# First blocks of 128, 128, 256, 256 and 256 tokens in a two-layer gated network behind a dynamic convolution, with earlier decoding of the weights and a new plan

## The chip, the core and the metric

One core of one Trainium2 chip runs the kernel. Its engines are TensorE (PE, with its weight loads shown apart as PEld), VectorE (DVE), ScalarE (ACT), GpSimd (POOL) and SyncE (SP, which here only issues transfers). The metric is the device time of one execution in microseconds, the median of the runs.

## What is computed

8192 tokens of 192 values pass through three steps. A causal convolution over 7 tokens has weights of its own for every token and head (a softmax of `weight_gen`). Then come two layers of 192 to 2048 to 192, the first with a rational function between its products, the second with a clipped product:

```python
def _moe_ref(x, w_in, w_out, a, b):
    h = x @ w_in
    h2 = h * h
    h3 = h2 * h
    P = a[0] + a[1] * h + a[2] * h2 + a[3] * h3
    Q = 1.0 + np.abs(b[0]) * np.abs(h) + np.abs(b[1]) * h2
    return (P / (Q + 1e-06)) @ w_out

def _moe2_ref(x, w_in, w_out):
    h = x @ w_in
    g = h * np.clip(h + 3.0, 0.0, 6.0) / 6.0
    return g @ w_out
```

The weights of both layers come as float64 and are decoded to float32 on the core.

## The kernel before

The tokens lie as 128 partitions of 64 rows, and a block is some of these rows for all partitions: `BL` (L46) has two blocks of 256 tokens and 15 of 512, called b0 to b16 here. A slice is the part of a block's 2048 hidden values that fills one 512-column bank: two groups of 128 hidden values for 256 tokens, one for 512. So a block of 256 has 8 slices and one of 512 has 16.

For a block the steps are these. The convolution's products (`conv_mul`, L171, on POOL, the first also on DVE) and sums (`conv_sum`, DVE) make the input; `xT` transposes it on PE, and `x_hi` (ACT) and `x_lo` (DVE) split it into a rounded part and a rest, since the products run on split operands. `in1` (L295) multiplies a slice of layer one with five matrix multiplications per group of 128 hidden values. The rational function takes a chain on ACT, DVE and POOL that ends with `pool_m` and `pool_lo` on POOL (L378, L389), which writes `glo`. Its denominator has two forms: `whole` slices add it up on DVE (L321), the others (through `act_u`, the Abs form) multiply it on POOL (L341). `out1` (L407) adds the slice to the block's output in the bank pair `y1`, again with five multiplications per group. When the last slice is in, `mid_y`, `mid_f`, `mid_head`, `head_lo`, `mid_tail` and `tail_lo` (L227 to L265) fold the output and split it for layer two: `in2` (L427), `act_r2`, `dve_g2`, then `out2` (L447) on unsplit float32, and `evac` to the output. `y1` is single, so the next block's `out1` waits for `tail_lo`.

The weights come in 28 jobs (`order`, L642): a load into one of `ST` = 8 buffers, then `low` and `scale` (ACT, or DVE for scale), `join` and `sign` (DVE), and for all but `o2` a cut into `hi` (ACT) and `lo` (POOL or DVE, L532). The first two loads are issued from ACT's queue, the others from SP's.

The order on every engine is written out by `plan()` (L820): a list scheduler with a cost and a due time for each step, made of the constants at L600 to L630 (`T` is the period of a slice). Engines take their instructions strictly in that order. Where PE has nothing to do in the plan, `idle_mm` (L398) puts in filler multiplications of the identity; on the chip they run in their place, whether the gap is there or not.

Of the kernel before, what the change touches and what calls it, by code (L numbers as in the profile page):

```python
# [8 lines left out]
F32 = mybir.dt.float32  # L9
# [10 lines left out]
def kernel(  # L20
# [12 lines left out]
    nc = tc.nc  # L33
# [12 lines left out]
    BL = [2, 2] + [4] * 15  # L46
    B0 = [sum(BL[:b]) // 2 for b in range(len(BL))]
    BT = [n * P for n in BL]
    BV = [n // 2 for n in BL]
    BF = [GW // n for n in BT]  # L50
    BMAX = max(BT)
    UB = [(b, v) for b, n in enumerate(BV) for v in range(n)]
# [52 lines left out]

    def load_chunk(c):
        t = two.tile([P, ROWS, D], F32, tag="x", name="x")
        first = c * CT - (K - 1)
        neg = max(0, -first)
        cut_at = ROWS - 2 if c == 0 else ROWS  # L110
        segs = [(0, P, neg, cut_at)]
# [7 lines left out]
        for p0, p1, r0, r1 in segs:  # L119
            src = bass.AP(  # L120
                tensor=xf.tensor,
                offset=xf.offset + (first + p0 * R + r0) * D,
                ap=[[R * D, p1 - p0], [1, (r1 - r0) * D]],
            )
            nc.sync.dma_start(out=t[p0:p1, r0:r1].rearrange("p r d -> p (r d)"), in_=src)
        xch[c] = t
# [36 lines left out]
    NS = 3  # L163
# [7 lines left out]
    def conv_mul(u, i, z, e="DVE"):  # L171
        eng = nc.vector if e == "DVE" else nc.gpsimd
        c, t = divmod(u * 2 + i, CT)
# [25 lines left out]
    def x_dup(u):  # L199
        t = xc[u]  # L200
        nc.scalar.activation(out=t[:, :, D:], in_=t[:, :, P:D], func=AF.Copy)

    def xT(u):
        t = xc.pop(u)
        ps = bank(("xT", u), [P, 2, HB], "xT")
        for s in range(2):
# [4 lines left out]
    def x_hi(u):  # L211
        b, v = UB[u]
        if v == 0:
            xin[0, b] = [
                two.tile([P, 2, BMAX], F32R, tag=n, name=n)[:, :, : BT[b]] for n in ("xh0", "xl0")
            ]
        xh = xin[0, b][0]
        nc.scalar.activation(out=xh[:, :, v * HB : (v + 1) * HB], in_=xps[u], func=AF.Copy)

    def x_lo(u):  # L220
        b, v = UB[u]
        xh, xl = (t[:, :, v * HB : (v + 1) * HB] for t in xin[0, b])
# [4 lines left out]
    def mid_y(b):  # L227
        ysb[b] = one.tile([P, BMAX], F32, tag="ys", name="ys")[:, : BT[b]]
        for h in range(2):
            nc.scalar.activation(  # L230
                out=ysb[b][h * 64 : (h + 1) * 64],
                in_=y1[b][(1 - h) * 64 : (2 - h) * 64, 1, : BT[b]],
# [3 lines left out]
    def mid_head(b):  # L236
        n = BT[b]
# [711 lines left out]
```

## Time and profile before

| | us |
|---|---|
| median of 3 runs | 1306.07 (1305.97 to 1306.53) |
| the profiled execution | 1305.82 |
| its span, first to last instruction | 1304.0 |
| PE busy, share of the span | 1281.1, 98% |
| DVE, ACT, POOL busy | 1143.5, 1069.3, 984.3 |
| granted TensorE clock, mean | 0.996 |

PE's instructions are pipelined, so a busy PE isn't a PE at its best: two multiplications that overlap count once, and one that runs at half clock counts fully. What PE achieves is read from the distance between starts. A filler counts as busy too. An instruction of float32 on unsplit operands stands twice in the trace (fillers and `out2`), a transpose once.

### The profile page before, as it was taken

Reading aid. Unit: us, or ns where it says so; the run is one execution under the profiler, and the core shown is the slowest. Engines: PE = TensorE matmul, PEld = TensorE weight load, DVE = VectorE, ACT = ScalarE, POOL = GpSimd, SP = SyncE. Lnnn points to the kernel's source line nnn. Section 1 sums busy time; section 2 is a strip of 40 time slices with the busy share of each in tenths; the row PEclk is TensorE's granted clock in tenths of the full one; section 3 lists DMA queues with packets and bytes.
Section 4 is the critical chain, followed back from the end, with each engine's and each line's share of the span. In section 5 each row is a group of like instructions: output and inputs, shape, how many; then the busy total and the mean of one; then the engine's idle time right before and its main releaser. Section 6 shows DMA issues by size and latency. Waiting matters only on the chain.

```text
span 1304.0 us, 18918 instructions
## 1 busy us (share of the span) xinstructions
PE 1281.1 (98%) x6640; PEld 1127.2 (86%) x6640; DVE 1143.5 (88%) x1774; ACT 1069.3 (82%) x1893; POOL 984.3 (75%) x811
## 2 busy tenths in 40 slices
PE   8889999999999999999999999999999999999998
PEld 8888878888889888898988889898888988888898
DVE  7899999999899898988989898898989889896931
ACT  6998989889788797978879798887979888797931
POOL 7998897978878787777968777787877778575620
PEclk9989999999999999999999999999999999999999
DMA  7440100110100101010010101001010000000000
GB/s 237 147 144 1 37 11 1 41 37 5 36 12 7 40 1 47 1 37 10 8 40 1 47 1 37 10 8 40 1 43 1 7 7 7 8 1 13 1 13 13
DMA packets 16263, 37.64 MB, mean 29 GB/s; under 512 B 1964, under 2 KB 12586, under 8 KB 16168
## 3 DMA queue, kind: packets, MB, share of 16 engines
q1 hardware_dynamic: 15864, 35.39, 8.3%
q10 hardware_dynamic: 304, 1.05, 0.3%
q8 instruction: 52, 0.85, 0.3%
q14 instruction: 43, 0.35, 0.1%
HBM read 30.14 MB, written 6.29 MB: 28 GB/s over the span
## 4 chain that ended last, share of the span: by engine, by line
PE 85%; ACT 7%; DVE 3%; POOL 2%; DMA 1%; issue 1%; SPq 0%; POOLq 0%; ACTq 0%
PE h L279 41%; PE y L454 24%; PE y L418 4%; PE y L421 4%; PE y L419 4%; PE y L420 4%; PE y L422 4%; ACT r L361 1%; ACT l L334 1%; ACT st L511 1%; ACT ys L230 1%; ACT r L356 1%; ACT w L316 1%; PE xT L207 1%; ACT v L311 1%
## 5 line engine op out<-in xcount | busy, mean ns | idle before, releaser
L389 POOL TENSOR_TENSOR glo<-w,r 128x512 fp32r<-128x512 f32 x256 | 331.0, 1295 | 186.5 <-PE y L422 113.5
L378 POOL TENSOR_TENSOR w<-w,ghi 128x512 f32<-128x512 f32 x256 | 330.9, 1295 | 44.1 <-DVE ghi L370 32.0
L454 PE MATMUL y<-wo,g 128*128 128x192 f32 x2048 | 352.1, 326 | 0.0
L454 PEld LDWEIGHTS y<-wo,g 128*128 128x128 f32 x2048 | 337.9, 190 | 8.5
L382 DVE SCALAR_TENSOR_TENSOR w<-h,acol,w 128x512 f32<-128x512 f32 x256 | 190.2, 744 | 34.1 <-POOL w L378 33.2
L437 ACT ACTIVATE g<-h 128x512 f32<-128x512 f32 x256 | 153.7, 600 | 71.1 <-PE h L279 69.0
L279 PE MATMUL h<-xh,wst 128*128 128x512 f32 (+1 forms) x544 | 206.1, 379 | 1.3 <-POOL wst L532 1.3
L279 PE MATMUL h<-xl,wst 128*128 128x512 f32 (+1 forms) x544 | 205.7, 378 | 0.1
L334 ACT ACTIVATE l<-h,acol 128x512 f32<-128x512 f32 x256 | 200.5, 783 | 2.5 <-PE h L279 2.5
L177 POOL TENSOR_TENSOR prod<-x,wk 128x672 f32<-128x672 f32 x127 | 189.4, 1503 | 17.3 <-DVE xc L192 12.1
L370 DVE SCALAR_TENSOR_TENSOR ghi<-h,acol,r 128x512 fp32r<-128x512 f32 x256 | 189.8, 744 | 10.9 <-PE y L420 3.9
L441 DVE SCALAR_TENSOR_TENSOR g<-g,h 128x512 f32<-128x512 f32 x256 | 174.1, 680 | 22.3 <-ACT g L437 20.7
L349 DVE SCALAR_TENSOR_TENSOR h<-l,acol,h 128x512 f32<-128x512 f32 x256 | 191.1, 749 | 2.4
L345 DVE TENSOR_TENSOR l<-h,l 128x512 f32<-128x512 f32 x256 | 174.0, 682 | 8.0 <-ACT l L334 4.7
L356 ACT ACTIVATE r<-w 128x512 f32<-128x512 f32 x256 | 161.2, 634 | 19.4 <-DVE w L321 15.3
L361 ACT ACTIVATE r<-r 128x512 f32<-128x512 f32 x256 | 161.7, 633 | 2.5
L321 DVE SCALAR_TENSOR_TENSOR w<-w,v 128x512 f32<-128x512 f32 x171 | 116.1, 679 | 22.3 <-ACT w L316 21.3
L311 ACT ACTIVATE v<-h,bab 128x512 f32<-128x512 f32 x171 | 112.9, 660 | 21.4 <-PE h L279 18.9
L316 ACT ACTIVATE w<-h,root 128x512 f32<-128x512 f32 x171 | 117.9, 690 | 7.8 <-DVE l L345 6.5
L279 PEld LDWEIGHTS h<-xh,wst 128*128 128x128 f32 x544 | 103.1, 189 | 20.8 <-POOL wst L532 1.5
L279 PEld LDWEIGHTS h<-xl,wst 128*128 128x128 f32 x544 | 102.9, 189 | 19.7 <-DVE xl L262 0.4
L341 POOL TENSOR_TENSOR w<-w,u 128x512 f32<-128x512 f32 x85 | 109.8, 1292 | 12.3 <-ACT w L327 10.6
(82 smaller groups left out, 2452.0 us busy)
## 6 DMA issues: line engine op xcount, KB each, us to landing
x<-in_x_dram SPq DMA_DIRECT2D x14, 960.0 KB, 4.7
st<-in_moe_w_out_dram SPq DMA_DIRECT2D x16, 384.0 KB, 3.3
out_dram<-osb SPq DMA_DIRECT2D x32, 192.0 KB, 1.8
st<-in_moe_w_in_dram SPq DMA_DIRECT2D x7, 512.0 KB, 4.7
wg<-in_weight_gen_dram SPq DMA_DIRECT2D x16, 112.0 KB, 2.0
st<-in_moe_w_in_dram SPq DMA_DIRECT2D x6, 256.0 KB, 4.1
x<-in_x_dram SPq DMA_DIRECT2D x1, 768.0 KB, 6.3
st<-in_moe_w_in_dram ACTq DMA_DIRECT2D x2, 256.0 KB, 5.7
```

The source lines that it names most:

```text
L177: eng.tensor_tensor(out=pr.rearrange("p (h g) k -> p k h g", g=G), in0=xch[c][:, t : t + K, hs].rearrange("p k (h g) -> p k h g", g=G), in ...
L279: nc.tensor.matmul(out=dst, lhsT=l[:, fs], rhs=r, start=(n == 0), stop=(n == len(seq) - 1), skip_group_check=True,)
L334: nc.scalar.activation(out=l, in_=h1[sl], func=AF.Identity, scale=acol[:, 3:4], bias=acol[:, 2:3])
L349: nc.vector.scalar_tensor_tensor(out=h, in0=e["l"], scalar=acol[:, 1:2], in1=h, op0=ALU.add, op1=ALU.mult)
L356: nc.scalar.activation(out=r, in_=e["w"], func=AF.Ln, bias=0.0 if whole(sl) else CEPS)
L361: nc.scalar.activation(out=r, in_=r, func=AF.Exp, scale=-1.0)
L370: nc.vector.scalar_tensor_tensor(out=ghi, in0=h, scalar=acol[:, 0:1], in1=e["r"], op0=ALU.add, op1=ALU.mult)
L378: nc.gpsimd.tensor_tensor(out=m, in0=m, in1=g1[sl][0].bitcast(F32), op=ALU.mult)
L382: nc.vector.scalar_tensor_tensor(out=m, in0=h1.pop(sl), scalar=acol[:, 0:1], in1=m, op0=ALU.add, op1=ALU.subtract)
L389: nc.gpsimd.tensor_tensor(out=glo, in0=e["m"], in1=e["r"], op=ALU.mult)
L441: nc.vector.scalar_tensor_tensor(out=g, in0=g, scalar=1.0, in1=h2.pop((b, q)), op0=ALU.min, op1=ALU.mult,)
L454: nc.tensor.matmul(out=y2[b, v][:, s, :], lhsT=g2[b, q][:, c : c + P], rhs=wo2[:, n, :], start=(n == 0 and s == 0), stop=(n == NF - 1), sk ...
```

## The change

- The blocks are now 128, 128, 256, 256, 256 and 14 of 512 tokens (b0 to b18). A block of 128 has 4 slices of four groups each, and its multiplications have 128 columns.
- `y1` becomes two tiles, `ya` and `yc`: a wide block has its head in one and its tail in the other, freed by `head_lo` and `tail_lo` apart; a block of 128 has both in one tile, and the two such blocks use a tile each.
- The order of the jobs takes layer one's weights first and in the order in which slices need them; a cut's rests are steps of their own; the due times of the jobs (`JP0`, `JPT`, `JPU`) stand closer together.
- The first x transfers are three instead of six; the last two rows of chunk 0 have a step of their own, and the memset of row 64 stands behind the transfer. The loads on ACT's queue stand ahead of the first exponential.
- `whole` takes half of the first 32 slices and two thirds of the others, where it took two thirds of all: 165 slices instead of 171.
- All constants of the plan are new, the bank limit of the small class is 4 instead of 3, and each part of `out2` waits only for the slices that it reads.

```diff
-    BL = [2, 2] + [4] * 15
-    B0 = [sum(BL[:b]) // 2 for b in range(len(BL))]
+    PRE = [1, 1, 2, 2, 2]
+    BL = PRE + [4] * ((R - sum(PRE)) // 4)
+    R0 = [sum(BL[:b]) for b in range(len(BL))]
...
-    UB = [(b, v) for b, n in enumerate(BV) for v in range(n)]
+    UB = [(b, v, R0[b] + 2 * v, min(2, n)) for b, n in enumerate(BL) for v in range(BV[b])]
...
     def load_chunk(c):
...
-        if neg:
-            for b in range(B):
-                p = b * S // R
-                nc.gpsimd.memset(t[p : p + 1, 0:neg, :], 0.0)
-                segs += [(p + 1, p + 16, 0, neg), (p + 16, p + S // R, 0, neg)]
-        if cut_at < ROWS:
-            segs.append((0, P, cut_at, ROWS))
...
+        if neg:
+            nc.gpsimd.memset(t[0:1, 0:neg, :], 0.0)
+            load_x(c, 16, P, 0, neg)
+            load_x(c, 1, 16, 0, neg)
+        load_x(c, 0, P, neg, ROWS if c else ROWS - 2)
+        for b in range(1, B if neg else 0):
+            nc.gpsimd.memset(t[b * P // B : b * P // B + 1, 0:neg, :], 0.0)
+
+    def load_rest():
+        load_x(0, 0, P, ROWS - 2, ROWS)
...
     def whole(sl):
-        return sl < QN and sl % QK in QS
+        return sl % QK in QS if sl < QE else sl % QL in QT
...
     def open_y1(b):
-        if b not in y1:
-            y1[b] = ps_y.tile([P, 2, GW], F32, tag="y1", name="y1")
+        if b in y1:
+            return
+        n = BT[b]
+        if tight(b):
+            tag = "ya" if b % 2 == 0 else "yc"
+            t = ps_y.tile([P, GW], F32, tag=tag, name="y1")
+            y1[b] = [t[:, :n], t[:, n : 2 * n]]
+            spare[b] = [t[:, GW - P :]]
+        else:
+            ts = [ps_y.tile([P, GW], F32, tag=tag, name="y1") for tag in ("ya", "yc")]
+            y1[b] = [t[:, :n] for t in ts]
+            spare[b] = [t[:, GW - P :] for t in ts if n < GW]
...
-    QN = 256
-    QK = 3
+    QE = 32
+    QK = 4
     QS = [0, 1]
+    QL = 3
+    QT = [0, 1]
...
+        ("pair", 0, 0), ("in", 0, 0), ("in", 0, 1), ("o1", 0), ("o1", 1), ("pair", 0, 2),
+        ("in", 0, 2), ("o1", 2), ("o1", 3), ("in", 0, 3), ("o1", 4), ("o1", 5), ("o1", 6),
+        ("o1", 7), ("pair", 1, 0), ("in", 1, 0), ("in", 1, 1), ("pair", 1, 2), ("in", 1, 2),
+        ("o2", 0), ("o2", 1), ("in", 1, 3), ("o2", 2), ("o2", 3), ("o2", 4), ("o2", 5),
+        ("o2", 6), ("o2", 7),
...
-            step("lo", flex, 0, "hi")
+            for i, m in enumerate({"in": [512], "pair": [512, 512], "o1": [256, 128]}[key[0]]):
+                cp, cd = 0.06 + m * 0.00234, 0.08 + m / 960
+                step(i, (("POOL", cp, 0.0), ("DVE", cd + 0.2, PEN)), 0, "hi")
...
-            take=[("y1", 1, [("head_lo", b), ("tail_lo", b)])] if q == 0 else [])
+            take=[] if q else [("ya" if b % 2 == 0 else "yc", 1, [("head_lo", b), ("tail_lo", b)])]
+            if tight(b) else [("ya", 1, [("head_lo", b)]), ("yc", 1, [("tail_lo", b)])])
```

In the new order PE has 480 multiplications of 128 columns, 720 of 256 and 3360 of 512 on split operands (before 0, 480 and 3600), as many `out2` and transposes as before, and 187 fillers (192).

On PE, where block 0's first output multiplication stands: before, behind the last multiplications of its fourth slice,

```order
L279 MATMUL h_449<-xl_234,win0hi 128x256
L279 MATMUL h_449<-xh_233,wst_82 128x256
L279 MATMUL h_449<-xl_234,wst_82 128x256
L279 MATMUL h_449<-xh_233,win0lo 128x256
L418 MATMUL y_168<-ghi,wo1h 128x256
L419 MATMUL y_168<-ghi,wo1l 128x256
L420 MATMUL y_168<-ghi,wo1s 128x256
L421 MATMUL y_168<-glo,wo1h 128x256
```

and now, behind the first slice of block 1 (`h_579`), with the transposes of block 2's first rows between them:

```order
L275 MATMUL h_579<-xh_355,wst_82 128x128
L275 MATMUL h_579<-xl_356,wst_82 128x128
L275 MATMUL h_579<-xh_355,win0lo 128x128
L212 MATMUL xT<-ident,xc 128x128
L213 MATMUL xT<-ident,xc 128x128
L212 MATMUL xT<-ident,xc 128x128
L213 MATMUL xT<-ident,xc 128x128
L414 MATMUL y_168<-ident 128x128 x5
L430 MATMUL y_168<-ghi,wo1h 128x128
L431 MATMUL y_168<-ghi,wo1l 128x128
L432 MATMUL y_168<-ghi,wo1s 128x128
```

The output multiplications have 128 columns instead of 256, and PE has taken in all four slices of block 0 and one of block 1 by then.

On POOL, its first instructions after the identity, before:

```order
L103 MEMSET ex 128x32
L115 MEMSET x 1x1152 x2
L177 TENSOR_TENSOR prod<-x,wk 128x7x96 x4
L532 TENSOR_TENSOR wst_82<-st,wst_82 64x512 x2
L532 TENSOR_TENSOR win0lo<-st,win0hi 128x512
L177 TENSOR_TENSOR prod<-x,wk 128x7x96
L532 TENSOR_TENSOR win0lo<-st,win0hi 128x512
L177 TENSOR_TENSOR prod<-x,wk 128x7x96
L532 TENSOR_TENSOR win0lo<-st,win0hi 128x512
L177 TENSOR_TENSOR prod<-x,wk 128x7x96
L378 TENSOR_TENSOR w<-w,ghi 128x512
L389 TENSOR_TENSOR glo<-w,r_312 128x512
```

and now:

```order
L105 MEMSET ex 128x32
L122 MEMSET x 1x1152
L127 MEMSET x 1x1152
L544 TENSOR_TENSOR wst_82<-st,wst_82 64x512
L181 TENSOR_TENSOR prod<-x,wk 128x7x96 x4
L544 TENSOR_TENSOR win0lo<-st,win0hi 128x512
L544 TENSOR_TENSOR wo1l<-st,wo1h 128x256
L544 TENSOR_TENSOR wo1s<-st,wo1s 128x2x64
L181 TENSOR_TENSOR prod<-x,wk 128x7x96
L544 TENSOR_TENSOR wo1l<-st,wo1h 128x256
L544 TENSOR_TENSOR wo1s<-st,wo1s 128x2x64
L181 TENSOR_TENSOR prod<-x,wk 128x7x96
```

The first half of the cut of `wst` moved ahead of the convolution's products, and cuts of layer one's output weights (`wo1l`, `wo1s`) stand between those products; before, the first `glo` came as the last of these rows, and now it stands 20 rows further on.

On ACT, its first instructions, before:

```order
L902 ACT_TABLE_LOAD
L142 ACTIVATE ex<-wg 128x32x7
L475 DMA st<-in_moe_w_in_dram 64x1024 x2
L475 DMA st<-in_moe_w_in_dram 128x1024
L796 ACTIVATE bab<-bcol 128x2
L511 ACTIVATE st<-st 128x512
L507 ACTIVATE dt<-st 128x512
L802 ACTIVATE root<-root 128x1
```

and now:

```order
L938 ACT_TABLE_LOAD
L487 DMA st<-in_moe_w_in_dram 64x1024 x2
L487 DMA st<-in_moe_w_in_dram 128x1024
L146 ACTIVATE ex<-wg 128x32x7
L523 ACTIVATE st<-st 128x512
L519 ACTIVATE dt<-st 128x512
L523 ACTIVATE st<-st 128x512
L519 ACTIVATE dt<-st 128x512
L543 ACTIVATE wst_82<-st 64x512 x2
L543 ACTIVATE win0hi<-st 128x512
L832 ACTIVATE bab<-bcol 128x2
```

The three loads moved ahead of the exponential `ex`, and `bab`, which reads the coefficients `bcol`, moved behind the decoding of the first two jobs.

## Rows read from the trace of the kernel before

**Rows 1.** The page, part 1: busy us, share of the span, instructions.

```profile
PE 1281.1 (98%) x6640; PEld 1127.2 (86%) x6640; DVE 1143.5 (88%) x1774; ACT 1069.3 (82%) x1893; POOL 984.3 (75%) x811
```

**Rows 2.** By stage: length, then PE, PEld, DVE, ACT, POOL busy, granted clock, DMA.

```profile
20.00:80.00 60.00, 51.61 (x418) 48.74 (x416) 54.91 (x91) 57.50 (x116) 58.12 (x60) 1.00 0.53 169
80.00:120.00 40.00, 37.64 (x258) 34.64 (x259) 38.22 (x66) 38.55 (x73) 33.62 (x29) 0.92 0.17 52
120.00:190.00 70.00, 69.75 (x389) 62.71 (x388) 69.39 (x109) 62.70 (x113) 64.26 (x54) 1.00 0.07 22
190.00:200.00 10.00, 7.24 (x23) 5.25 (x24) 9.48 (x15) 8.75 (x16) 9.42 (x8) 0.83 0.00 0
```

**Rows 3.** By stage, PE's instructions on the identity alone: length, busy (count), clock.

```profile
20.00:120.00 100.00, 33.50 (x272) 0.97 0.39 122
```

**Rows 4.** Timeline of PE: start and length in us, line, count merged.

```profile
23.77 0.28 PE L279 MATMUL h<-xh,win0lo 128*128 128x256 f32 x1
...
24.37 0.28 PE L279 MATMUL h<-xh,win0lo 128*128 128x256 f32 x1
24.49 2.28 PE L402 MATMUL y<-ident 128*128 128x128 f32 x19
```

**Rows 5.** The chain that ended last, its longest pieces: start, length, count.

```profile
1262.73 17.01 PE h L279 x75
1279.74 20.82 PE y L454 x128
```

**Rows 6.** PE's groups by form, 200 to 1240 us: count | busy, mean ns.

```profile
L454 PE MATMUL y<-wo,g 128*128 128x192 f32 x1689 | 291.6, 326 | 0.0
...
L208 PE MATMUL xT<-ident,xc 128*128 128x128 f32 x52 | 12.7, 272 | 0.0
```

**Rows 7.** Timeline of PE's weight loads around 32 us, behind a wait.

```profile
32.25 0.19 PEld L279 LDWEIGHTS h<-xh,wst 128*128 128x128 f32 x1 [1.53 <-POOL wst L532]
32.35 0.19 PEld L279 LDWEIGHTS h<-xl,wst 128*128 128x128 f32 x1
```

**Rows 8.** Timeline of POOL: first products, first cut, first and eighth glo.

```profile
7.61 5.09 POOL L177 TENSOR_TENSOR prod<-x,wk 128x672 f32<-128x672 f32 x3 [4.16 <-DMA x<-in_x_dram]
...
15.66 2.67 POOL L532 TENSOR_TENSOR wst<-st,wst 64x512 fp32r<-64x512 f32 x2 [0.89 <-POOL prod L177]
...
28.79 1.28 POOL L389 TENSOR_TENSOR glo<-w,r 128x512 fp32r<-128x512 f32 x1 [1.06 <-DVE w L382]
...
76.39 1.28 POOL L389 TENSOR_TENSOR glo<-w,r 128x512 fp32r<-128x512 f32 x1
```

**Rows 9.** POOL's groups by form, the whole run: count | busy, mean ns.

```profile
L177 POOL TENSOR_TENSOR prod<-x,wk 128x672 f32<-128x672 f32 x127 | 189.4, 1503 | 17.3 <-DVE xc L192 12.1 <-DMA x<-in_x_dram 4.2 <-DMA st<-in_moe_w_in_dram 0.6
L341 POOL TENSOR_TENSOR w<-w,u 128x512 f32<-128x512 f32 x85 | 109.8, 1292 | 12.3 <-ACT w L327 10.6 <-DVE h L349 1.6
L532 POOL TENSOR_TENSOR wst<-st,wst 64x512 fp32r<-64x512 f32 x8 | 10.4, 1302 | 1.3 <-POOL prod L177 0.9
L152 POOL TENSOR_TENSOR wk<-ex,sg 128x224 f32<-128x224 f32 x15 | 9.3, 617 | 0.7 <-DVE sg L147 0.7
...
L532 POOL TENSOR_TENSOR wo1l<-st,wo1h 128x256 fp32r<-128x256 f32 x8 | 6.0, 750 | 0.0
...
L532 POOL TENSOR_TENSOR wo1s<-st,wo1s 128x128 fp32r<-128x128 f32 x8 | 3.8, 469 | 0.0
```

**Rows 10.** Timeline of ACT: the wait for bcol, and b2's mid_y.

```profile
12.07 0.20 ACT L796 ACTIVATE bab<-bcol 128x2 f32<-128x2 f32 x1 [8.05 <-DMA bcol<-in_moe_b_dram]
...
191.43 1.20 ACT L230 ACTIVATE ys<-y 64x512 f32<-64x512 f32 x2
```

**Rows 11.** Timeline of PE: the first product, and waits at two block ends.

```profile
19.14 0.36 PE L279 MATMUL h<-xh,win0hi 128*128 128x256 f32 x1
...
80.08 0.58 PE L279 MATMUL h<-xh,win1hi 128*128 128x256 f32 x1 [1.25 <-ACT xh L242]
...
193.40 0.40 PE L279 MATMUL h<-xh,win0lo 128*128 128x512 f32 x1
196.10 0.79 PE L418 MATMUL y<-ghi,wo1h 128*128 128x512 f32 x1 [2.30 <-DVE xl L262]
```

**Rows 12.** Timeline of DVE: b2's tail_lo.

```profile
195.35 0.69 DVE L262 TENSOR_TENSOR xl<-y,xh 128x512 fp32r<-128x512 f32 x1
```

More of the change, by code (lines that the diff above doesn't have):

```diff
@@ L162 @@
     NH = 4
-    NS = 3
+    NS = 4
     def bank(key, shape, name):
@@ L400, in idle_mm @@
         open_y1(0)
-        for i in range(n):
+        to = spare[max(y1)]
+        for i in range(n if to else 0):
             nc.tensor.matmul(
-                out=y1[max(y1)][:, i % 2, GW - P :], lhsT=ident, rhs=ident,
-                start=first and i < 2, stop=False, skip_group_check=True,
+                out=to[i % len(to)], lhsT=ident, rhs=ident,
+                start=first and i < len(to), stop=False, skip_group_check=True,
             )
@@ L419, in out1 @@
             mm(out=a, lhsT=wo1l[:, n, :], rhs=gh, start=False, stop=False, **kw)
-            mm(out=c, lhsT=ws, rhs=gh, start=st, stop=False, **kw)
+            mm(out=c, lhsT=ws, rhs=gh, start=st and not tight(b), stop=False, **kw)
             mm(out=a, lhsT=wo1h[:, n, :], rhs=gl, start=False, stop=sp, **kw)
@@ L650, with step @@
     for n, key in enumerate(order):
-        p = JP0 + min(n, 14) * JPT + max(0, n - 14) * JPU - (30.0 if n < 2 else 0.0)
+        p = JP0 + min(n, 14) * JPT + max(0, n - 14) * JPU
         f64, split = WS == 2, key[0] != "o2"
         sz = 1.0 if key[0] in ("in", "pair") else 0.75
-        last = ("job", key, "lo" if split else "sign" if f64 else "load")
-        def step(k, eng, cost, prev, take=(), lat=None, also=[]):
-            op(
-                ("job", key, k), eng, cost, p - LP * (k == "load"), lambda e=None, key=key, k=k: job_step(key, k, e),
+        cuts = {"in": 1, "pair": 2, "o1": 2, "o2": 0}[key[0]]
+        last = [("job", key, n) for n in range(cuts)] or [("job", key, "sign" if f64 else "load")]
+        def step(k, eng, cost, prev, take=(), lat=None, also=[], n=n):
+            op(
+                ("job", key, k), eng, cost,
+                X0P + W0[n] if k == "load" and n < 2 else p - LP * (k == "load"), lambda e=None, key=key, k=k: job_step(key, k, e),
                 ([("job", key, prev)] if prev else []) + also, take, lat,
             )
-        flex = (("POOL", 1.25 * sz, 0.0), ("DVE", 0.62 * sz, PEN))
-        step("load", "SP", 2.0 * sz, None, [("big", ST, [last])] if f64 or split else [], 2.0)
+        step("load", "SP", 2.1 * sz, None, [("big", ST, last)] if f64 or split else [], 2.0)
         if f64:
@@ L726 @@
             f = (q + 1) * BF[b] - 1
-            jobs_in = [done["in", 1, f // 4], done["pair", 1, f // 8 * 2]]
+            jobs_in = [k for n in range(q * BF[b], f + 1)
+                       for k in done["in", 1, n // 4] + done["pair", 1, n // 8 * 2]]
             add("in2", "PE", cm, t2, in2, b, q, lat=0.2,
@@ L905 @@
         when = {o["key"]: (t0, t1) for o, _, t0, t1 in steps}
-        fold = [(when["mid_y", b][0], when["tail_lo", b][1]) for b in range(2)]
+        fold = [
+            (when["mid_y", b][0], when["tail_lo", b][1]) for b in range(len(BL)) if BT[b] < GW
+        ]
         last = 2.0
```

229 lines of the change are left out of this document (117 added, 112 removed).

## Prediction

> **What bounds the kernel now.** I read the page first: PE is busy for 98% of the span [rows 1]. That is a share over the whole run, so next came the table by stage [rows 2]. From 120 us on PE is full but for ten microseconds around 195 and the last few. Before 120 us it is not: it stands idle for 10.7 of the 100 us from 20 to 120 (60 − 51.61 and 40 − 37.64), while DVE, ACT and POOL are nearly full. And part of its busy time there is filler: of 384 halves of idle_mm's multiplications (192 of them, each stands twice), 272 fall between 20 and 120 us [rows 3]. So there are two stages: a start in which the three elementwise engines set the pace and PE pads, and from 120 us a long stage in which PE's own queue sets the end. A change helps if it shortens the padded start by more than it adds to PE's queue.
>
> For the second, PE's queue needs prices, from start to start [rows 4]. A 256-column multiplication costs (24.37 − 23.77)/5 = 0.120 us, half a filler (2.28 − 0.28)/18 = 0.111 (19 of them, the last one's length taken off, 0.28 as in the row above), and so a filler 0.222; a transpose I set at 0.11 like it, since it has the same 128 columns. From the chain's longest pieces [rows 5] come 17.01/75 = 0.227 at 512 columns and 20.82/128 = 0.162 for half of an output multiplication of layer two (0.163 with the last one's end, 0.161 without). The queue of before is then 3600 x 0.227 + 480 x 0.120 + 2048 x 0.162 + 128 x 0.11 = 817.2 + 57.6 + 331.8 + 14.1 = 1220.7 us. The span is 1304.0, so 83.3 us are not work. The prices hold: the 3301 + 1689 + 104 instructions (512 columns, output halves, transposes, by the grouped view of that stretch, first and last of its 16 rows in [rows 6]) from 200 to 1240 us come to 749.3 + 273.6 + 11.4 = 1034.3 of 1040, which leaves 5.7 us for waits and rounding in 1040.
>
> **What the change adds to PE's queue.** Blocks of 512 tokens fall from 15 to 14, those of 256 rise from 2 to 3, and two of 128 come in. Each block takes 240 multiplications on the split weights whatever its width. So 240 x 0.227 = 54.5 goes, 240 x 0.120 = 28.8 comes, and 480 multiplications of 128 columns come whose price no row shows. The low bound is streaming alone: half of the 0.107 between 256 and 512 columns, taken off 0.120, is 0.0665. The high bound is the 256-column price, 0.120. I take 0.11, from the weight loads: every multiplication has its own load, and after a wait the next load begins 0.10 to 0.11 us after the first (32.25 and 32.35, [rows 7]), with 128 columns each. At 256 columns streaming hides the load; at 128 it can't. 480 x 0.11 = 52.8 (bounds 31.9 and 57.6), so the queue grows by **27.1 us** (6.2 to 31.9), to 1247.8. What the trace shows is one load's pace; the Trainium skill, in "TensorE: Matmul & The Clock Gate", section "Back-to-back issue gap", gives 81 ns for a multiplication of 128 columns in a stream of loads and multiplications, and 131 ns at 512. The trace has 227 ns for the latter, so the pair doesn't fit these operands; with 81 ns the growth would be 13 us and the streaming rival below would hold.
>
> **What it takes from the start.** The output of a 128-token block is complete after 4 slices, not 8, so layer two begins earlier; in return the decoding of the weights stands ahead of the first slices. I follow POOL, which is busy for 58.12 of the 60 us from 20 to 80 [rows 2]. Before, its first glo ends at 28.79 + 1.28 = 30.1 us and the eighth, the last of block 0, at 76.39 + 1.28 = 77.7 [rows 8]. In the new order one convolution product (1.50), three halves of wst (1.30 each) and eight pairs of wo1l and wo1s (0.75 + 0.47) more stand ahead of the first glo: 15.2 us at the groups' means [rows 9]. POOL also starts later: the first cut of wst now stands before the convolution products, which began at 7.61 as x landed. That cut needs the weights and ACT's steps. Before, ACT stood until 12.07 for bcol, and the cut began at 15.66, 3.6 us later [rows 8, 10]; now the loads are issued ahead of the exponential and the decoding stands ahead of bcol, so I set the cut at 13, some 2.7 sooner, and the products at 14.3: 6.7 us later, 1.3 of them the cut already counted. First glo: 30.1 + 15.2 + 5.4 = **50.7 us**. The block's first input still reaches PE near 19.5, as before (19.14, [rows 11]): the products are later, but two are enough, not four.
>
> From 19.5 PE has 100 multiplications of 128 columns, 6 transposes and 79 fillers before the first output multiplication: 11.0 + 0.7 + 17.5 = 29.2, so it would be there at 48.7 and waits to 50.7. To the block's fourth slice it has 140 multiplications and 39 fillers, 15.4 + 8.7: it ends at 74.8. POOL is done earlier: against the eighth glo of before it has four each of w and glo fewer (10.3 at 1.29 and 1.28), four products fewer (6.0), one half of wst more (1.3), and one product of the Abs form (1.3), one wk (0.6) and two memsets (0.3) fewer: 77.7 − 17.2 + 5.4 = 65.9. From here PE is the later one, by 9 us, and that is what the smaller blocks lead to: **PE's own queue becomes the bound at about 50 us instead of 120**.
>
> The other edits. The single memset of row 64 waits for the first x transfer, with the wst cut and the products behind it on POOL; the products need that x anyway, and the cut comes later than it, so nothing. Three x transfers fewer ahead of the coefficients shorten SP's list, and nobody waits for the coefficients once ACT decodes first. The rest of chunk 0 goes behind a weight load; it is needed by the third row, later. More slices on the Abs form (91 against 85, 16 of 32 at first) move a DVE step of each to POOL and ACT, which have slack once PE binds. Two output tiles let a first output multiplication go after head_lo, but the third in a slice waits for tail_lo: at most two of 0.227.
>
> **The sum.** From the first output multiplication at 50.7 PE has 380 x 0.11 + 720 x 0.120 + 3360 x 0.227 + 2048 x 0.162 + 120 x 0.11 = 41.8 + 86.4 + 762.7 + 331.8 + 13.2 = 1235.9, and 49 fillers, 10.9. Waits: 6 us for the price check's remainder over the run; at block 0 about 1, as at 80.08 before (1.25 for the head's copy, [rows 11]); at the first 512-block about 2, since there, as before 196.10 (2.30), only layer one's products stand beside a chain of 4.6 us from mid_y to tail_lo, 195.35 + 0.69 − 191.43 [rows 10 to 12]; 1 elsewhere. From the last start to the end of the span 3.8 us, as before (1304.0 − 1300.56 + 0.33, [rows 5]). Together 50.7 + 1235.9 + 10.9 + 10 + 3.8 = 1311.3, against 1304.0: not-work falls by some 20 us, the queue grows by 27. The profiled execution took 1305.82 with a span of 1304.0, 1.8 outside, and the median is 1306.07, 0.25 above it. So **1313 us**.
>
> **Rivals.** (1) Not slower: the load doesn't limit 128 columns. For it: no row shows loads back to back without a long stream between them, and an unhindered one could be pulled further ahead. Against: the uncovered load. The Trainium skill's 81 ns above speaks for it too. It decides at about 0.09: below it PE arrives before its data and the elementwise engines bound as before. Block 0's tail_lo then falls near 72 (65.9, one slice of output, 1.3, and a chain of 4.6 or somewhat less). From there 156 DVE instructions lead to block 3's tail_lo; before, 190 took the 120 us from 80 to 200 [rows 2], 0.63 each: 170.5, and 1.1 for one slice of output that stands ahead of layer two's. PE's rest from there is 1120.6 by the same prices, with 6 + 2 + 3.8: a span of 1304.0, a time of 1306. At the pace of 80 to 120 alone (66 in 40 us, 0.606) it is 4 less, 1302, and with block 0 done 3 us sooner 1299. (2) The first output multiplication comes sooner: POOL isn't held by the cut and ACT feeds it, so that PE is there at 45 rather than 50.7. PE's own sum (48.7) speaks against more than 2 us of it unless x arrives earlier. 1307 to 1310. (3) PE waits in the new start as it did before: 1304.0 − 19.1 − 1220.2 (its queue but for four transposes) − 28.9 (130 fillers after the first product) − 3.8 − 6 = 26 us were lost there. If half of that returns, through the many block ends and a clock that falls to half as it did (0.92 in 80 to 120, 0.83 in 190 to 200, [rows 2]): 1322.
>
> **How the numbers follow.** The forecast has 0.64, (1) 0.18, (2) 0.10, (3) 0.08. A difference of 0.2% (2.6 us) is about what a measurement of this kernel can tell from none. Slower by more: 0.58 of the forecast, (3), and 0.04 of (2): 0.70. Within: 0.06 of the forecast, 0.06 of (2), 0.07 of (1): 0.19. Faster: 0.11, all from (1). Range: the terms that I set are the price at 128 columns (−21 to +5, the low end being rival 1), the first output (±4) and the waits (−3 to +12); 1303 to 1321 leaves out the faster part of (1) and the upper part of (3).
>
> **What would show it.** In the timeline of the new kernel, 128-column multiplications 0.11 us apart, with loads back to back; the first output multiplication near 50 us; few PE waits between 60 and 190; DVE no longer full at 120 to 190; not-work near 63 us. If they stand 0.07 apart, or PE still waits for glo and xl until 170 us, the forecast is wrong and (1) is right.

## The result, and the profile of the changed kernel

The changed kernel took **1320.84 us** (median of 4 runs, 1315.99 to 1322.48) against 1306.30 for the kernel before beside it (1305.97 to 1306.63): a ratio of 1.0105, 95% interval 1.0079 to 1.0132. It is 1.1% slower. The forecast was 1313, with a range of 1303 to 1321. Its four runs spread with the granted clock: the fastest had a mean of 0.994, the slowest 0.989, the other two 0.991.

The profiled execution took 1321.1 us with a span of 1319.3. Of the page, part 1, which answers [rows 1]:

```profile
PE 1310.3 (99%) x7110; PEld 1171.2 (89%) x7110; DVE 1152.2 (87%) x1778; ACT 1079.8 (82%) x1908; POOL 991.3 (75%) x816
```

The table by stage answers [rows 2]. Its columns are the stretch, its length, then busy time and count of PE, PEld, DVE, ACT and POOL, the granted clock, and the DMA share and rate. I cut it where the granted clock changes:

```profile
20.00:78.60 58.60, 57.83 (x512) 57.22 (x511) 49.16 (x83) 53.42 (x109) 50.55 (x53) 1.00 0.59 178
78.60:102.50 23.90, 23.90 (x115) 23.90 (x113) 12.37 (x22) 12.37 (x24) 10.39 (x12) 0.50 0.02 5
102.50:120.00 17.50, 16.90 (x142) 16.61 (x141) 11.84 (x22) 11.02 (x23) 11.63 (x10) 1.00 0.00 1
120.00:190.00 70.00, 69.77 (x554) 69.55 (x553) 68.37 (x111) 64.08 (x119) 64.12 (x52) 1.00 0.06 20
190.00:200.00 10.00, 10.00 (x81) 10.00 (x80) 9.20 (x14) 8.60 (x17) 9.45 (x8) 1.00 0.20 45
```

Two things stand in it. From 20 us on PE is full, where before it stood idle for 10.7 us of 100. Until 49 us that is partly filler: 79 of them, 17.5 us, stand between its first product and its first output multiplication, and without them (e4, below) it waits there. Behind that the elementwise engines are no longer the ones that are late. And for 23.9 us, from 78.6 to 102.5, the granted clock is half (1.2 GHz), with PE busy in all of it: it gets 115 instructions done, and DVE, ACT and POOL, full before in such a place, are half empty. In the kernel before there was one such stretch ahead of 120 us, 6.8 us long, and one of 3.4 us at its first 512 block:

```profile
79.60:86.40 6.80, 5.89 (x23) 5.17 (x24) 6.23 (x13) 6.39 (x14) 6.80 (x6) 0.50 0.28 85
195.70:199.10 3.40, 3.00 (x7) 2.42 (x8) 3.40 (x6) 3.40 (x7) 3.24 (x3) 0.50 0.00 0
```

The stretch isn't made of narrow multiplications alone. Ten of 256 columns, from 87.5 to 89.7 us, stand in the middle of it and run at the half level too; the clock is back only behind ten more and eight filler halves:

```profile
89.08 0.41 PE L275 MATMUL h<-xh,wst 128*128 128x256 f32 x1
89.30 0.41 PE L275 MATMUL h<-xl,wst 128*128 128x256 f32 x1
...
100.81 1.86 PE L414 MATMUL y<-ident 128*128 128x128 f32 x8
102.38 0.36 PE L430 MATMUL y<-ghi,wo1h 128*128 128x128 f32 x1
102.57 0.27 PE L431 MATMUL y<-ghi,wo1l 128*128 128x128 f32 x1
```

The timeline of PE shows the price of a 128-column multiplication at either level: 0.11 us from start to start at full clock, 0.21 at half (columns: start, length, line, operation).

```profile
60.07 0.28 PE L433 MATMUL y<-glo,wo1h 128*128 128x128 f32 x1
60.19 0.28 PE L434 MATMUL y<-glo,wo1s 128*128 128x128 f32 x1
...
90.68 0.41 PE L430 MATMUL y<-ghi,wo1h 128*128 128x128 f32 x1
90.89 0.41 PE L431 MATMUL y<-ghi,wo1l 128*128 128x128 f32 x1
91.11 0.41 PE L432 MATMUL y<-ghi,wo1s 128*128 128x128 f32 x1
```

Over all of them at full clock the distance has a median of 0.111 and a mean of 0.113; I take 0.112.

Of block 0, the first product, the first output multiplication and the last of the fourth slice, on PE, and the first and fourth glo on POOL (the second and third stand between them), beside which [rows 8] and [rows 11] stand:

```profile
19.58 0.30 PE L275 MATMUL h<-xh,win0hi 128*128 128x128 f32 x1
...
49.10 0.31 PE L430 MATMUL y<-ghi,wo1h 128*128 128x128 f32 x1
...
73.36 0.27 PE L434 MATMUL y<-glo,wo1s 128*128 128x128 f32 x1
...
47.19 1.29 POOL L386 TENSOR_TENSOR glo<-w,r 128x512 fp32r<-128x512 f32 x1
...
66.50 1.28 POOL L386 TENSOR_TENSOR glo<-w,r 128x512 fp32r<-128x512 f32 x1 [0.64 <-DVE w L379]
```

And PE's longest waits from 60 to 190 us (total, times, longest):

```profile
PE h L275 <- DVE g L453: 0.6, 1, 0.6
PE h L275 <- DVE xl L248: 0.6, 2, 0.3
```

So from 60 us on waits for data are gone almost wholly. What is new is the clock.

### The profile page after: what moved, and what is told of

It reads as the page before. It is cut to its first block, busy times and chain, and to the rows that moved or that the text cites. A ratio compares the mean times of both kernels' runs of the same rounds, so it can differ in the third digit from the quotient of the medians.

```text
span 1319.3 us, 19918 instructions
## 1 busy us (share of the span) xinstructions
PE 1310.3 (99%) x7110; PEld 1171.2 (89%) x7110; DVE 1152.2 (87%) x1778; ACT 1079.8 (82%) x1908; POOL 991.3 (75%) x816
## 4 chain that ended last, share of the span: by engine, by line
PE 97%; DVE 1%; DMA 1%; ACT 1%; issue 0%; ACTq 0%; DVEq 0%
PE h L275 46%; PE y L466 25%; PE y L432 5%; PE y L434 5%; PE y L433 5%; PE y L431 5%; PE y L430 5%; PE y L414 2%; DMA st<-in_moe_w_in_dram 1%; PE xT L212 1%; PE xT L213 1%; DVE xc L196 0%; DVE ghi L367 0%; DVE h L346 0%; ACT ys L233 0%
## 5 line engine op out<-in xcount | busy, mean ns | idle before, releaser
L375 POOL TENSOR_TENSOR w<-w,ghi 128x512 f32<-128x512 f32 x256 | 331.3, 1297 | 35.6 <-DVE ghi L367 27.3
L453 DVE SCALAR_TENSOR_TENSOR g<-g,h 128x512 f32<-128x512 f32 x256 | 174.7, 682 | 66.8 <-ACT g L449 65.9
L275 PE MATMUL h<-xh,wst 128*128 128x512 f32 (+2 forms) x608 | 221.2, 364 | 0.0
L275 PE MATMUL h<-xl,wst 128*128 128x512 f32 (+2 forms) x608 | 221.0, 363 | 0.2 <-DVE xl L248 0.2
L181 POOL TENSOR_TENSOR prod<-x,wk 128x672 f32<-128x672 f32 x128 | 190.4, 1509 | 30.2 <-DVE xc L196 23.9
L338 POOL TENSOR_TENSOR w<-w,u 128x512 f32<-128x512 f32 x91 | 117.9, 1295 | 37.3 <-ACT w L324 36.8
L275 PEld LDWEIGHTS h<-xl,wst 128*128 128x128 f32 x608 | 116.5, 192 | 18.6 <-DVE xl L248 0.4
L275 PEld LDWEIGHTS h<-xh,wst 128*128 128x128 f32 x608 | 116.4, 191 | 18.1
L308 ACT ACTIVATE v<-h,bab 128x512 f32<-128x512 f32 x165 | 107.7, 653 | 28.6 <-PE h L275 18.5
L275 PE MATMUL h<-xh,win0hi 128*128 128x512 f32 (+2 forms) x304 | 121.3, 399 | 0.2 <-DVE w L318 0.2
L318 DVE SCALAR_TENSOR_TENSOR w<-w,v 128x512 f32<-128x512 f32 x165 | 111.9, 678 | 7.5 <-ACT w L313 5.5
```

Source lines behind the costliest of these rows:

```text
L181: eng.tensor_tensor(out=pr.rearrange("p (h g) k -> p k h g", g=G), in0=xch[c][:, t : t + K, hs].rearrange("p k (h g) -> p k h g", g=G), in ...
L275: nc.tensor.matmul(out=dst, lhsT=l[:, fs], rhs=r, start=(n == 0), stop=(n == len(seq) - 1), skip_group_check=True,)
L375: nc.gpsimd.tensor_tensor(out=m, in0=m, in1=g1[sl][0].bitcast(F32), op=ALU.mult)
L453: nc.vector.scalar_tensor_tensor(out=g, in0=g, scalar=1.0, in1=h2.pop((b, q)), op0=ALU.min, op1=ALU.mult,)
```

## The experiments

The theory after the result: 480 multiplications of 128 columns, each bound by its weight load, lengthen PE's queue by some 27 us; and the stream of them, once the fillers thin out, is what the clock falls in, which costs another 11. Rivals: the clock falls there whatever PE runs, since layer two begins there; the fillers are what delays PE; the new plan and its early decoding cost by themselves. All medians are in us, "before" is the kernel before on the same chip, 1306.1 to 1306.4.

### Is it the weight load?

**e9, half the weight columns.** In both input products of the two 128-token blocks, four of five multiplications load only 64 weight columns; they stream 128 as always. The kernel leaves out the rest, so it doesn't compute the same output.

```diff
+            d, ls = dst, l[:, fs]
+            if n and dst.shape[1] == P:
+                d, ls = dst[:64], l[:, f * P : f * P + 64]
             nc.tensor.matmul(
-                out=dst, lhsT=l[:, fs], rhs=r, start=(n == 0), stop=(n == len(seq) - 1),
+                out=d, lhsT=ls, rhs=r, start=(n == 0), stop=(n == len(seq) - 1),
```

> The changed kernel, but of the five multiplications per group in both input products of the two 128-token blocks, the last four use only 64 of the 128 weight columns, so that their weight load is half as wide; the streamed columns stay 128. The correction terms of half the hidden values of these blocks are left out. 256 of 4560 multiplications are concerned. Theory (the weight load sets the 0.112 us at 128 columns): these stand 0.06 to 0.09 us apart. Rival (a multiplication of this kind takes 0.112 whatever its load): they stay at 0.11. The time itself decides nothing: by the theory up to 256 x 0.05 = 12.8 us less queue, but a shorter one gives the clock a lighter stretch; 1306 to 1322.

1301.02, ratio to before 0.9963 (0.9948 to 0.9978). The timeline of PE, where `128*64` is the loaded weight:

```profile
21.00 0.22 PE L278 MATMUL h<-xh,wst 128*64 128x128 f32 x1
21.06 0.22 PE L278 MATMUL h<-xl,wst 128*64 128x128 f32 x1
21.12 0.27 PE L278 MATMUL h<-xh,win0lo 128*64 128x128 f32 x1
21.23 0.28 PE L278 MATMUL h<-xh,win0hi 128*128 128x128 f32 x1
```

With half the load the next one starts 0.06 us later, not 0.11, with the same 128 columns streamed. So the load sets the price, and streaming would allow half of it. The granted clock is full from 6.7 us on: 128-column multiplications that follow each other faster went with a full clock. This run is also the forecast's first rival with its condition made true on about half of the multiplications: it gave 1299 to 1306 for that, and the time is 1301. But the rival's mechanism isn't there. It has PE arrive before its data, and in e9 PE waits for data 2.0 us in all from 60 to 190 us, the most of it on

```profile
PE h L278 <- DVE xl L248: 0.6, 2, 0.3
```

So PE's queue is the bound in e9 as well, and that the time lies in the rival's range is chance. From the changed kernel's side an estimate is 1320.8 less 13.3 of queue (256 x 0.052) and less the 10 to 11 us that the clock is worth (below), about 1297, 4 below the measured time.

The Trainium skill has this in "TensorE: Matmul & The Clock Gate", section "LDWEIGHTS (loading the stationary operand)": a load takes a time that goes with its weight columns, 106.7 ns for 128 and 53.3 for 64 as an estimate by its formula. The 0.112 and 0.060 us agree to within 7 ns. The 81 ns that the prediction cited from the section "Back-to-back issue gap" agree with no run here.

### Is it the stream of 128 columns that the clock falls in?

**e3, the same blocks with 256 columns.** The 128-token blocks read their columns twice, so that a multiplication streams 256; the copy is overwritten or not read.

```diff
+            if dst.shape[1] == HB and r.shape[1] == P:
+                r = r[:, None, :].to_broadcast([P, 2, P])
...
+            if tight(b):
+                gh, gl = (g[:, None, :].to_broadcast([P, 2, P]) for g in (gh, gl))
```

> The changed kernel in which the multiplications of the two 128-token blocks stream their 128 columns twice, 256 columns each (the copy is overwritten or not read; the output is the same; the last group of a slice in the two input products stays at 128). About 432 of 480 multiplications go from 0.112 to 0.120 us: 3.5 us more queue. Theory (PE streams for only half of each 0.112, and the clock falls after a long stretch of that once the fillers end): no long stretch at half clock, 12 us come back, 1321 + 3.5 - 12 = 1310 to 1314. Rival (the fall has nothing to do with the columns): the stretch from 78 to 102 us stays and the time is 1322 to 1326. If 256 columns cost the same as 128 in this stretch, the weight load is the limit there, as the prediction took it; if they cost 0.05 more, it isn't.

1313.76, ratio 1.0055 (1.004 to 1.007): 7 us less than the changed kernel, though every second column is waste. The same stretch as above, and the distance of the widened multiplications:

```profile
78.60:102.50 23.90, 23.90 (x205) 23.90 (x204) 18.11 (x32) 17.89 (x34) 16.73 (x15) 1.00 0.02 5
```

```profile
82.99 0.28 PE L277 MATMUL h<-xh,win1lo 128*128 128x256 f32 x1
83.10 0.28 PE L277 MATMUL h<-xh,win1hi 128*128 128x256 f32 x1
83.22 0.28 PE L277 MATMUL h<-xl,win1hi 128*128 128x256 f32 x1
```

In e3 the clock is full to the end, and 205 instructions run in the stretch instead of 115. Twice the columns cost 0.12 instead of 0.112. The trace has 400 widened multiplications (the expectation took 432), so with 3.2 us more queue (400 x 0.008) and 7.1 less time the clock was worth 10.3. The spread of the changed kernel says the same: from a mean clock of 0.994 to 0.989 over 1319 us the time at half clock grows by some 13 us, which would cost 6.5, and the times are 6.5 apart. (Only one of these runs has a trace, and e10's four, at 0.985 to 0.988, don't follow their clock, so this supports and doesn't prove.)

**e5 and e10, without the later fillers.** e5 is e3, and e10 the changed kernel, with fillers only until the first output multiplication of layer one, 54 fewer.

```diff
-                if t0 < when["in2", IB, 0][0] and n > 0:
+                if t0 < when["out1", 0][0] and n > 0:
```

> As e3 (the 128-token blocks stream 256 columns), with fillers only until the first output multiplication of layer one: 133 instead of 187, 54 fewer, 12.0 us of PE's queue. Theory (from the first output on PE's queue is the bound, and the wide multiplications alone keep the clock): the clock stays full and the time falls by 3 to 8 us against e3's 1313.8, to 1306 to 1311; not by all 12, since POOL ends the glo of the fourth slice at 75.4 us in the changed kernel and PE's output multiplication stood at about 79. Rival (those fillers only fill gaps): within 2 us of e3. Rival (they are what kept the clock): a stretch at half clock comes back, and 1318 or more.

> The changed kernel with fillers only until the first output multiplication (54 fewer), and the 128-token blocks as they are. With e3 and e5 this makes a table of two by two. e5 took 7.4 us off e3. Theory (a stream of 128-column multiplications alone lets the clock fall and doesn't raise it): the clock falls earlier than at 78 us, near 50 to 65, stays at half for 20 us or more, and the time is 1312 to 1322, at least 6 above e5's 1306.4. Rival (the fillers' 12 us are worth the same here as with wide multiplications): 1313 or less with a half-clock stretch that is no longer than 10 us.

e5: 1306.38, ratio 1.0003 (0.9994 to 1.0013). e10: 1315.55, ratio 1.0074 (1.0057 to 1.0091).

| | with all fillers | with the early ones only |
|---|---|---|
| 128 columns | 1320.84 | 1315.55 (e10) |
| 256 columns, half of them copies | 1313.76 (e3) | 1306.38 (e5) |

In both, PE waits for DVE until about 55, where fillers had stood, and the clock falls within 1.1 us of the next start. First e5, then e10:

```profile
54.97 0.38 PE L277 MATMUL h<-xh,win0hi 128*128 128x256 f32 x1 [3.13 <-DVE w L385]
```

```profile
55.38 0.33 PE L275 MATMUL h<-xh,win0hi 128*128 128x128 f32 x1 [3.60 <-DVE w L379]
```

By stage, again first e5:

```profile
56.00:59.40 3.40, 3.40 (x18) 3.40 (x17) 2.91 (x5) 3.40 (x7) 3.32 (x3) 0.50 0.29 89
```

```profile
55.70:83.00 27.30, 27.30 (x130) 27.30 (x129) 15.60 (x29) 16.79 (x33) 17.19 (x19) 0.50 0.39 129
```

In e5, on widened multiplications, the clock is back after 3.4 us. In e10 it stays at half for 27.3 us in which PE has no gap at all, on 128-column multiplications, and comes back at the end of the first ten of 256 columns (block 2's first slice; the timeline of PE, where the distance goes from 0.21 to 0.09):

```profile
82.57 0.42 PE L275 MATMUL h<-xl,wst 128*128 128x256 f32 x1
82.79 0.40 PE L275 MATMUL h<-xh,win0lo 128*128 128x256 f32 x1
83.00 0.24 PE L275 MATMUL h<-xh,win1hi 128*128 128x128 f32 x1
83.09 0.33 PE L275 MATMUL h<-xl,win1hi 128*128 128x128 f32 x1
```

So here what streams, and not whether PE is occupied, decides how long the clock stays at half once it has fallen. Net of what they do to the clock, the later fillers cost 5 to 7 us of the 12 that they occupy: PE's queue is the bound behind the first output, as the prediction has it, and 3.1 to 3.6 of the rest are the wait that now stands in their place. (The expectations of e4 and e5 take a glo that ends at 75.3 and an output multiplication at 79 for block 0's fourth slice. They are block 1's first; block 0's fourth glo ended at 67.8 and its output ran from 71.2 to 73.6.)

**e4, no fillers at all.** The condition above is made never true.

> The changed kernel without the 187 filler multiplications. After the first output multiplication 49 of them stand in PE's queue, 10.9 us, and 79 before it, 17.5 us. Theory (PE's queue is the bound from 50 us on): the start until the first output stays near 49 us, since the first glo ends at 48.5, and at most 4 us come back until the fourth slice, whose glo ends at 75.4; but PE waits more, the clock is half for longer than 24 us, from 20 us on, and the time is 1322 to 1340. Rival (the fillers only delay PE and do nothing for the clock): the half-clock stretch stays at 24 us or less, and the time is 1310 to 1318.

1316.18, ratio 1.0088 (1.0063 to 1.0113). The expectation of 1322 or more failed: the theory's long time at half clock came, but the time is the rival's (1310 to 1318). The trace has no record of the clock ahead of 83.1 us, but the distances are those of the half level: 0.21 for 128 columns and 0.21 for 256.

```profile
80.72 0.41 PE L434 MATMUL y<-glo,wo1s 128*128 128x128 f32 x1
80.94 0.52 PE L275 MATMUL h<-xh,win0hi 128*128 128x256 f32 x1
81.26 0.41 PE L275 MATMUL h<-xl,win0hi 128*128 128x256 f32 x1
81.47 0.42 PE L275 MATMUL h<-xh,wst 128*128 128x256 f32 x1
```

The whole start from the first product at 18.6 us ran at half, and it came back behind ten multiplications of 256 columns, as in e10. That this is 5 us faster than the changed kernel fits where it runs at half. Until 49 us PE waits for its data in any case, and the first output multiplication starts at 50.8 us against 49.1. From 49.0 to 83.1 PE is full for 34.1 us with 160 instructions, which is an estimated 16 us of work lost against 11 in the changed kernel; in return the 10.9 us of fillers are gone.

### What do the blocks cost, and what is the rest of the change worth?

**e1, e2 and e11: other first blocks** in the changed kernel: four of 256 tokens, two (as before), six.

```diff
-    PRE = [1, 1, 2, 2, 2]
+    PRE = [2, 2, 2, 2]
```

> The changed kernel with first blocks of 256, 256, 256, 256 tokens instead of 128, 128, 256, 256, 256; the plan's constants, job order, tiles and transfers stay. PE's queue loses 480 multiplications at 0.112 and 720 - 960 = -240 at 0.120, so 53.8 us go and 28.8 come: 25 us less. Theory (the 128-column multiplications lengthen the queue by their load and bring the long stretch at half clock): no granted clock of half for longer than 10 us before 120 us, and the time falls by 15 us or more, to 1295 to 1306; what keeps it from the full 25 + 12 is that block 0 needs eight slices from POOL again. Rival (the clock falls at that place whatever the width, because layer two begins there): a stretch of 20 us or more at half clock stays and the time is 1300 to 1310. Rival (the new plan and its early decoding cost by themselves): 1310 or more.

> The changed kernel with the block sizes of the kernel before (256, 256, then 15 of 512); everything else of the change stays. PE's queue is that of before, 1220.7 us. Theory (the blocks are what costs, the rest of the change is worth a little): 1300 to 1308. Rival (the rest of the change, plan and order of decoding, is worth much, and the small blocks spoil it): under 1300. Rival (the rest costs): over 1310.

> The changed kernel with six first blocks of 256 tokens and 13 of 512. Against e1 (four) PE's queue grows by 480 x 0.120 - 240 x 0.227 = 3.1 us. Theory (from about 105 us on e1 is bound by PE's queue alone, so nothing is left to gain by a later first 512 block): 1304.5 to 1308. Rival (e1 still loses some at its first 512 block): 1300 to 1303.

e1: **1303.40**, ratio 0.9977 (0.9967 to 0.9986), 17.4 us below the changed kernel and 0.2% below the kernel before, a small difference that the interval still keeps apart from none. Its one stretch at half clock in the start is 3.4 us long. e2: 1313.74, ratio 1.0055 (1.0038 to 1.0072), above the 1308 that the theory gave. e11: 1305.77, ratio 0.9993 (0.9984 to 1.0003), 2.4 above e1 where the queue grows by 3.1: a later first 512 block has next to nothing left to give e1.

**e7, e12: late decoding.** e7 is the changed kernel with the job order of before and later due times; e12 the kernel before with four first blocks of 256.

```diff
-    JPT = 0.491
+    JPT = 2.744
-    ORD = 1
+    ORD = 0
```

```diff
-    BL = [2, 2] + [4] * 15
+    BL = [2, 2, 2, 2] + [4] * 14
```

> The changed kernel with the order of the weight jobs of before (layer two's first jobs between layer one's) and the later due times of the first jobs (JPT 2.744 instead of 0.491). The blocks stay. PE has 29.8 us of queue before the first output multiplication instead of 42. Theory (decoding the weights ahead of the slices is what delays the first output to 49 us, and the 128-token blocks do the rest): first output at 37 to 44 us, but PE then waits for weights, several us in one place, and the time is 1316 to 1330. Rival (early decoding loses as much as it gains): 1305 to 1316.

> The kernel before with four first blocks of 256 tokens instead of two, all else as it was. PE's queue grows by 3.1 us. In the kernel before PE waits until 120 us and loses 5 us more at the first 512 block, near 196. Theory (what e1 gained over e2, 10 us, was that the first 512 block comes later): 1300 to 1306. Rival (that gain needs the early decoding of the weights): 1307 to 1315.

e7: 1327.56, ratio 1.0171 (1.0155 to 1.0186). Its first output multiplication starts at 37 us, as the theory said, and then PE waits for DVE, which is still decoding weights (the waits of PE, 80 to 130 us; `wo` are layer two's output weights):

```profile
PE h L275 <- DVE wo L536: 6.7, 3, 4.2
PE xT L212 <- DVE w L379: 3.1, 1, 3.1
```

Its clock is at half too, in three stretches of 23.9 us together between 96.4 and 127.1, as long as in the changed kernel. So the 6.7 us between the two aren't a longer time at half clock.

e12: 1316.25, ratio 1.0080 (1.0065 to 1.0095). That is above the theory's range and at the rival's upper end. So neither the blocks nor the rest of the change is faster than the kernel before alone; four blocks of 256 and the rest together are (e1). Blocks of 128 without early decoding run into the decoding; the rest of the change with two blocks of 256 loses 7 us to before; four blocks of 256 without it lose 10. Only e7 takes the order of decoding and its due times by themselves, so which part of the rest e1 needs isn't shown. Where e12 loses its 10 us can be estimated: take the work that PE has started by a time, at the prediction's prices, off that time. Of what is not work e12 has 73.7 us by 190 us, the kernel before 68.6, so its start is 5 us longer. At its first 512 block (270 to 300 us, a wait of 2.2 for the rest of the tail) it loses some 4, as the kernel before does at 190 to 200, and some 2 more near 328; and its queue is 3.1 longer. Why its start is longer wasn't tested.

**e6, e8: the later fillers of e1 and e2** left out, by the same line as in e5.

> As e1 (first blocks 256, 256, 256, 256) with fillers only until the first output multiplication: 141 instead of 223. In e1 the elementwise engines set the pace until about 100 us (DVE 19.7 and 19.96 of 20 from 80 to 120), so there the fillers lie in gaps. Theory (fillers in gaps cost nothing and hold the clock): the half-clock stretch grows beyond e1's 3.4 us and the time is 1303 to 1312. Rival (they delay PE here too): 1296 to 1301.

> As e2 (first blocks 256, 256 as in the kernel before) with fillers only until the first output multiplication: 130 instead of 273. e2 was 7.4 us slower than the kernel before with the same queue of work. Theory (the many fillers of that plan, 65.5 us against 46, delay PE): 1303 to 1308. Rival (the elementwise engines' start is later because all weights are decoded first, and the first 512 block comes too early for them): 1311 to 1316, with PE standing idle where the fillers were.

e6: 1303.22, ratio 0.9976 (0.9965 to 0.9987). e8: 1314.36, ratio 1.0062 (1.0047 to 1.0077). Neither differs from e1 and e2. By stage, e1 and then e6:

```profile
60.00:80.00 20.00, 17.04 (x140) 16.46 (x140) 18.32 (x33) 18.96 (x37) 18.99 (x19) 1.00 0.43 142
80.00:110.00 30.00, 27.29 (x213) 26.94 (x214) 29.69 (x52) 29.34 (x56) 27.68 (x25) 0.94 0.02 5
```

```profile
60.00:80.00 20.00, 12.96 (x83) 11.86 (x81) 18.27 (x33) 18.96 (x37) 18.61 (x21) 0.82 0.47 159
80.00:110.00 30.00, 25.60 (x175) 24.90 (x175) 29.70 (x52) 29.33 (x55) 27.60 (x25) 0.83 0.02 5
```

PE has less to do and a lower clock in e6, and the busy time of DVE, ACT and POOL is the same to 0.4 us: there the elementwise engines set the pace, so 82 fillers and 24 us more at half clock together cost and give nothing that the medians show. Each by itself wasn't tested, and within e6 the run with the lowest mean clock (0.988) took 1304.5 us and the one with the highest (0.993) 1301.9. In e8 it is the same, with PE busy for 7.8 us of the 20 from 40 to 60; so e2's loss isn't fillers. Its first output multiplication starts at 45 us, against 35 in the kernel before, and its first product of layer two at 100.7 against 80.1: this fits the first half of the rival, that decoding everything first delays a start that the elementwise engines bound (the plan, tiles and transfers changed with it, and no run takes them apart in e2). Its second half doesn't hold: by the estimate just used e2 has 78.2 us of not-work by 120 us against 67.9 before, and at the first 512 block (200 to 250 us) it loses 5.4, about as the kernel before does (4.8). All of e2's loss lies in the start.

## Why the prediction was nearly right, and where it wasn't

Step by step:

- **The price at 128 columns.** Taken at 0.11 from two weight loads behind a wait [rows 7]; it measured 0.112, and e9 shows the load as its cause. The queue grew by 28, not 27.
- **The start.** First product at 19.5, measured 19.58; first output multiplication at 50.7, measured 49.1; end of block 0's fourth output at 74.8 on PE and 65.9 on POOL, measured 73.6 and 67.8. Until here the sum was 1 to 2 us high. The wait that it has before the first output isn't there: the first glo ended at 48.5 and not at 50.7, and PE came to its output multiplication at 49.1 by its own queue, forecast for 48.7. PE's own queue did become the bound at about 50 us: e5 and e10 get 5 to 7 us from fillers behind that point, where e6 and e8, bound by the elementwise engines, get nothing.
- **The mis-sized term: 10 us of waits** behind the first output. From the measured pieces it is 1319.3 − 49.1 − 1236.7 − 10.9 − 3.8 = 18.8 us (1236.7 is the work behind the first output at 0.112). Of it 11 are the clock: the 23.9 us at half hold 80 multiplications of 128 columns, 20 of 256 and 12 filler halves, 12.7 us at full clock. The remaining 8 are close to the 10 taken; block 0's end is 1.6 of them where I took 1, and the first 512 block, near 292 us, loses about 1 where I took 2 (its two output multiplications wait for a rest of the split input, 0.2 and 0.5, against 2.30 in [rows 11]). e3 puts the clock at 10.3 by another way. So the time falls within the range by 0.2 us, and by luck: the clock had no term in the sum, and the allowance of up to 12 us on the waits, made for waits, took it in. Two of the four runs lie above the range.
- **What the prediction missed.** It knew that a load hides half of the streaming at 128 columns and it listed the clock, but in its third rival, as a thing that comes with PE's waits. What came just before is as the rival has it: at block 0's end, from 74.6 to 76.8, PE loses 1.6 us over four multiplications, and 2 us later the clock is at half; whether it would have fallen without that loss isn't shown. But e3 loses as much there (1.7, from 75.7) and holds the clock, and in the kernel before a wait of 1.25 at block 0's end [rows 11] stood beside a stretch at half of 6.8 us, not 23.9. The narrow multiplications are what e3 takes away, and with them the stretch goes: from 69.0 us to 78.6 PE ran 60 of 128 columns and 10 of 256, no filler, and in the 23.9 us then 80 more. What ended the stretch in the changed kernel stays open, since ten of 256 columns stood in its middle as well. I had the count of fillers ahead of and behind the first output and used it only as a length to add. That rival's 1322 was near the time, but put most of the loss into waits that didn't come back.
- **What would show it.** Three of five signs came: 0.11 us between 128-column multiplications, the first output near 50, few waits from 60 to 190. "DVE no longer full at 120 to 190" did not: it is busy for 68.37 of 70, and PE is full all the same, so a full DVE didn't mean that it was late. Not-work is 1319.3 − 1248.8 = 70.5, not 63; the clock, 11 us, is more than the gap.
- **The first rival** fell by its condition, the price (0.112, and it decides at 0.09), and e9 met its time when the condition was made on half of the multiplications, but with PE's queue as the bound and not the elementwise engines, so by chance. **The second** was right in direction, by 1.6 us.

In terms of work and not-work, the prices as in the prediction (128 columns at 0.112, widened multiplications at 0.120):

| | span | queue | not work |
|---|---|---|---|
| before | 1304.0 | 1220.7 | 83.3 |
| changed | 1319.3 | 1248.8 | 70.5 |
| e3, 256 columns | 1310.6 | 1252.0 | 58.6 |
| e5, and early fillers only | 1305.5 | 1252.0 | 53.5 |
| e1, four blocks of 256 | 1300.4 | 1223.8 | 76.6 |
| e2, two blocks of 256 | 1312.3 | 1220.7 | 91.6 |

The change does shorten the start, by 13 us as it stands and by 30 in e5. It pays for it with 28 us of weight loads for half-filled multiplications. e1 gives up about half of the shorter start and all but 3 us of that price, and with e6, which has the same blocks, is the one version with the full output that beats the kernel before, by 0.2%.

## What to carry to other kernels

Halving a block to start the next stage earlier saves waiting in the start but keeps the number of weight loads; once the stream is shorter than the load, compare the whole extra load time with what the start can give back, which here was 28 us against 13, and 31 against 30 in the best version with these blocks (e5). Read the clock beside what PE streams, not beside its busy share: a PE that is full of narrow multiplications sat at half clock here, and filling them with useless columns was 7 us faster (e3). And fillers and stretches at half clock cost 5 to 11 us here where PE's own queue was the bound, and next to nothing where the elementwise engines were (e6): ask first which engine is late in that stretch.

## What was not expected of the hardware

- At half clock a multiplication costs 0.213 us with 128 columns and with 256 alike; at full clock 0.112 and 0.120. That fits a load that takes longer at half clock too; no run halves the load there.
- A stream of mostly 128-column multiplications on split operands without a gap did not bring the clock back (23.9 us at half in the changed kernel, 27.3 in e10, until 83.1 in e4). In e10 and e4 ten multiplications of 256 columns came just ahead of its return; in the changed kernel ten of them, from 87.5 us, didn't bring it, and ten more with eight filler halves came just ahead of it; on widened ones (e5) it was back after 3.4 us, and behind the same loss at block 0's end (e3) it didn't fall. Fillers have 128 columns too, but each of their halves takes 0.112 us at full and 0.213 at half clock, and the clock rose under them within the first 7.2 us of every run that had them.
- Stretches at half clock came to some 27 us in the start of e6, and its median is that of e1 with 3.4 us of them.
